# A Fourier mixing layer and a SoLU feed-forward on one Trainium2 core: when the last chunk of a batch pair is transformed, and the order of work in the opening

## Chip, core and metric

One core of a Trainium2 chip runs the whole program. The metric is the device time of one execution in microseconds (us). Engines: TensorE (PE, its weight loads PEld), VectorE (DVE), ScalarE (ACT), GpSimd (POOL) and SyncE (SP), which here only issues DMAs.

## What is computed

```python
X = np.fft.fft(np.fft.fft(x, axis=1), axis=2).real      # x: (8, 3136, 256) float32
h = X.reshape(25088, 256) @ w_in                          # w_in: (256, 1024)
e = np.exp(h - h.max(-1, keepdims=True))
solu = h * e / (e.sum(-1, keepdims=True) + 1e-9)
ln = (solu - mean(solu)) / np.sqrt(var(solu) + 1e-6) * g_ln   # over the 1024 features
out = ln @ w_out                                          # w_out: (1024, 256)
```

The weights arrive as 64-bit floats and are turned into 32-bit floats on the chip.

## The kernel before, in words

**Tiling.** The eight batches go in four pairs (`Pair`, p = 0 to 3, called the first to the fourth). The sequence of 3136 is split as 49 x 64. A pair is loaded in eight chunks (`load`, L117): SyncE brings `xa`, GpSimd's indirect DMA brings `xb`, the rows of the mirrored positions; the last chunk has one more row, `x0`. `add_mirror` (L136) adds the two and `fold` or `fold_part` (L152, L164) adds and subtracts mirrored features into `y`; columns 0 and 128 of `y`, its edges, are copied. `transform1` (L184) does one half of a chunk: four matmul instructions into a PSUM bank (six for the last half, which has `x0` too), a ScalarE copy to `z`, and after a chunk's second half a DMA of `z` to `zd` in DRAM (`keep`). `turn` (L226) reads `zd` back as `g`, five of the 25 values of k1 at a time, in four DMAs.

**Units.** A unit is one k1 of one pair; there are 100 of them, `units[i]`, and the main loops run one step i per unit. `transform2` (L234) makes q of unit i + 2 from g in step i, and `spread` sends one row of it as `r` over SyncE. `up` (L267) multiplies q with Wi (w_in after the feature transform) into two PSUM tiles; `even` (L275) and `join` (L281) on VectorE make h and its extreme, `expo` (ScalarE), `product` (VectorE), `square` (ScalarE) follow. `turn_both` transposes 32 x 32 blocks on VectorE, and `move_blocks` (L396) moves the blocks of two units with 16 DMAs on SyncE in every even step. Five steps later (`lag`) the unit is multiplied with w_out in seven half-size products (`Down`), whose sums GpSimd makes a step ahead (`sums`, L433). `power`, `store` and the loads of later chunks are on GpSimd's queue too; each engine works through its instructions in the order in which they are written.

**Order of the next pair's work.** While a pair's units run, the next pair is loaded and transformed. `SUMS` (L698) holds for each pair the step at which each chunk's mirror begins: f + 2c, with f = 3, 27, 53 for pairs 1, 2, 3. In `ahead` and `ahead_pe` the step a = i - SUMS[p][c] decides: mirror halves at a = 0 and 1, fold halves at 1 and 2, the load of chunk c + 2 at 2, the two halves of `transform1` at 3 and 4. GpSimd's mirrors and sums wait (`behind`) for VectorE's last product, since both read two operands from SBUF. `turn_parts` issues g's first part of pair p in step 25p - 4.

**Opening.** Before unit 0 the first pair goes through without units beside it: the loop at L761 takes the eight chunks, mixed with the conversion of w_in (four pieces: `exponent_in`, `confine`, `narrow_in`) and later w_out (four pieces: `exponent_out`, `confine`, `narrow_out`). `confine` takes three ScalarE instructions (or two of VectorE with `here`). `product_in(h)` (L654) multiplies the feature transform with w_in: h = 0 even half, h = 1 odd half, h = KD the middle column (`w_mid`), and copies the result from PSUM to SBUF by ScalarE. Steps 0 to 4 (`WHOLE`) have a loop of their own (L840), with TensorE transposes in place of block moves.

Of the kernel before, what the change touches and what calls it, by code (L numbers as in the profile page):

```python
# [25 lines left out]
CH = 4  # L26
NC = NH // CH
# [16 lines left out]
def kernel(  # L44
# [19 lines left out]
    nc = tc.nc  # L64
# [3 lines left out]
    KD = D // P  # L68
# [83 lines left out]
    def fold(pr, c):  # L152

        xa, _, x0 = pr.raw.pop(c)
        pr.y[c] = xpool.tile([PR, CH, D], FP32, tag="y", name="y")
        sides = [(pr.y[c], xa)]
        if c == NC - 1:
            pr.y0 = xpool.tile([PR, 1, D], FP32, tag="y0", name="y0", bufs=1)
            sides.append((pr.y0, x0))
        for o, i in sides:  # L160
            fold_features(o, i)
            nc.vector.tensor_copy(out=o[:, :, 0:129:128], in_=i[:, :, 0:129:128])  # L162

    def fold_part(pr, c, part):  # L164

# [447 lines left out]
    class Weights:  # L613
# [40 lines left out]
        def product_in(self, h):  # L654
            ps = ps_h.tile([P, FF], FP32, tag=f"h{h % 2}", name="wps")
            for half in range(2):
                fs = slice(half * HW, (half + 1) * HW)
                for c in range(KD):
                    lhsT = self.m[:, c, :] if h == KD else self.Q[:, c, h * P : (h + 1) * P]
                    nc.tensor.matmul(ps[:, fs], lhsT, self.w_in[c][:, fs], start=(c == 0), stop=(c == KD - 1))  # L660
            nc.scalar.copy(w_mid if h == KD else Wi[:, h, :], ps)

        def place_out(self):
# [31 lines left out]

    SUMS = [None] + [[f + 2 * c for c in range(NC)] for f in (3, 27, 53)]  # L698

    def ahead(pr, i, work, after=None):  # L700

# [12 lines left out]
                          mybir.DependencyInfo(mybir.DependencyClass.Sync, mybir.DependencyReason.DATA),  # L714
                          reason="two operands at a time from SBUF")

    def ahead_pe(pr, i):

        for c in range(NC):
            half = i - SUMS[pr.p][c] - 3  # L720
            if half in (0, 1):
                transform1(pr, c * CH // 2 + half)

# [6 lines left out]
    with tc.manual_schedule():  # L730
        pairs = [Pair(p) for p in range(NP)]
        first, weights = pairs[0], Weights()
# [25 lines left out]
            nc.vector.memset(t, 0.0)  # L758
        weights.exponent_in(0)
        weights.exponent_in(1)  # L760
        for c in range(NC):  # L761

            if c == 0:
                weights.narrow_in(0)
                weights.narrow_in(1)
            elif c < 3:
                weights.narrow_in(c + 1)
            if c < 2:
                weights.exponent_in(c + 2)
            add_mirror(first, c, nc.vector)  # L770
            fold(first, c)
            if c == NC - 1:
                for i in range(3):
                    weights.exponent_out(i)
            if c + 6 < NC:
                load(first, c + 6)
            if c == 3:
                weights.place_out()
                for i in range(2):
                    weights.load_out(i)  # L780
                weights.load_table(0)
                weights.mid()
                weights.scale_out()
            for s in range(CH // 2):
                transform1(first, c * CH // 2 + s)
            if c == 3:
                weights.product_in(0)

        turn(first, 0, nc.sync, 0, 2)
        turn(first, 0, nc.gpsimd, 2, KG)  # L790

        confine(weights.units[0], True)
        for i in range(1, 3):
            confine(weights.units[i])
        weights.product_in(1)
        weights.narrow_out(0)
        weights.exponent_out(3)
        weights.product_in(2)
        for i in range(1, 3):
            weights.narrow_out(i)  # L800

        units = [Unit(p, k1) for p in range(NP) for k1 in range(NK)]
        for t in units[:2]:
            take2(t, transform2(pairs[0], t.k1))
            spread(t)
        confine(weights.units[-1])
        for c in (2, 3, 0, 1, 4, 5, 6, 7):
            keep(first, c, slice(4 * KG, ZR))
        weights.load_table(1)
# [30 lines left out]
        for i in range(whole + 1):  # L840
            cur = units[i]
            prv = units[i - 1] if i else None
            if prv:
                turn_whole(prv)
            for s in cur.signs:
                join(cur, s)
            if prv and i < whole:
                for o, ps in prv.wait:
                    nc.vector.tensor_copy(out=o, in_=ps)
            for s in cur.signs:  # L850
                expo(cur, s)
            if prv and i == whole:
                for o, ps in prv.wait:
                    nc.scalar.copy(o, ps)
            if i == 0:

                weights.narrow_out(3)
            for s in cur.signs:
                product(cur, s)
                if i < whole and s == 0:  # L860
                    square(cur, s)
            if i == 1:
                weights.centre()
                weight_sums()
            if i < whole:

                begin(i + 1)
                if 1 in cur.signs:
                    square(cur, 1)
                stats(cur)  # L870
                power(cur)
            else:
                for s in cur.signs:
                    square(cur, s)
                other_pairs(i, ahead, "mirror", cur)
                turn_both(cur)
                stats(cur)
                power(cur)
            if i == 0:
                turn(first, 1, nc.sync)  # L880
            for work in ("mirror", "fold", "load") if i < whole else ("fold", "load"):
                other_pairs(i, ahead, work)

        def by_seven(i):
# [6 lines left out]
        for i in range(whole + 1, len(units) + lag + 1):  # L891
            cur = units[i] if i < len(units) else None
            prv = units[i - 1] if whole < i - 1 < len(units) else None
            old = units[i - lag] if i < len(units) + lag else None
            seven = by_seven(i - lag)
            kept = units[i - lag - 1] if i >= lag + 1 else None

            if kept:
                store(kept, 0)
            if cur:  # L900
                enter(i)
                even(cur, up(cur, 0))
                cur.odd = up(cur, 1)
                second_transform(i + 2)
            if seven:
                new = Down(old, fresh)
                fresh = False
                new.p1()
                new.seed()
            if i == len(units):  # L910
                for s in prv.signs:
                    square(prv, s)
            if prv:
                stats(prv)
            if seven:
                new.p4()
                new.p5()
                new.keep_p()
            elif old:
                plain = [(s, down(old, s, result(s + 1)[:, 0:D])) for s in old.signs]  # L920
            if cur:
                other_pairs(i, ahead_pe)
            if seven:
                new.p6()
                new.keep_x()
                new.p2()
                new.keep_c()
            elif old:
                for s, ps in plain:
                    scale(old, s, ps)  # L930
            if prv and prv.batch.shared and prv.w:
                prv.batch.mix()
            if cur:
                for s in cur.signs:
                    join(cur, s)
            if seven:
                new.p3()
                new.p7()
                new.finish()
            if cur:  # L940
                other_pairs(i, ahead, "mirror")
            if by_seven(i + 1 - lag):
                sums(units[i + 1 - lag], prv, nc.vector if i > len(units) else nc.gpsimd)
            if i % 2 == 0 and whole < i - 1 < len(units) - 2:
                batches[i // 2 - 1].place()
                move_blocks(batches[i // 2 - 1], slice(0, 2))
            if prv:
                power(prv)
            if kept and 1 in kept.signs:
                store(kept, 1)  # L950
            if cur:
                other_pairs(i, ahead, "fold")
                for s in cur.signs:
                    expo(cur, s)
                for s in cur.signs:
                    product(cur, s)
                if i < len(units) - 1:
                    for s in cur.signs:
                        square(cur, s)
                turn_both(cur)  # L960
                if cur.p == 0 and i in (5, 8, 11):
                    turn(first, (i + 1) // 3)
                for pr in pairs[1:]:
                    turn_parts(pr, i - pr.p * NK)
                other_pairs(i, ahead, "load")
            if i in (len(units), len(units) + 1):
                w = i - len(units)
                if w == 0:
                    batches[-1].place()
                move_blocks(batches[-1], slice(w, w + 1), (nc.sync, nc.gpsimd) if w else (nc.sync,))  # L970
# [82 lines left out]
```

## Time and profile before

| | us |
|---|---|
| median of 3 runs (1149.79 to 1153.33) | 1151.1 |
| profiled execution | 1150.92 |
| its span | 1149.1 |
| TensorE busy | 1098.1 |
| VectorE busy | 993.0 |
| ScalarE, GpSimd busy | 799.3, 799.9 |
| mean granted TensorE clock | 0.994 of full |
| busy TensorE in eleven stretches of 10 us, 0 to 110 | 0.00, 1.96, 5.51, 9.22, 9.43, 9.07, 8.75, 9.61, 8.05, 8.45, 7.05 |

The span runs from the first to the last instruction; the execution's time is 1.8 us longer. In the lines of a timeline the columns are start, length, engine, line of the kernel, operation, output <- input, shape and count; in brackets the idle time of the engine ahead of it and what ended it. In the lines of waits they are engine, tile and line that waited, <- what ended the wait, then total us, count and longest. A queue's own issue of DMAs stands under SPq, or under POOL for GpSimd.

### The profile page before, as it was taken

Reading aid. Unit: us, or ns where it says so; the run is one execution under the profiler, and the core shown is the slowest. Engines: PE = TensorE matmul, PEld = TensorE weight load, DVE = VectorE, ACT = ScalarE, POOL = GpSimd, SP = SyncE. Lnnn points to the kernel's source line nnn. Section 1 sums busy time; section 2 is a strip of 40 time slices with the busy share of each in tenths; the row PEclk is TensorE's granted clock in tenths of the full one; section 3 lists DMA queues with packets and bytes.
Section 4 is the critical chain, followed back from the end, with each engine's and each line's share of the span. In section 5 each row is a group of like instructions: output and inputs, shape, how many; then the busy total and the mean of one; then the engine's idle time right before and its main releaser. Section 6 shows DMA issues by size and latency. Waiting matters only on the chain.

```text
span 1149.1 us, 21936 instructions
## 1 busy us (share of the span) xinstructions
PE 1098.1 (96%) x7026; PEld 877.3 (76%) x7026; DVE 993.0 (86%) x1440; ACT 799.3 (70%) x1945; POOL 799.9 (70%) x698
## 2 busy tenths in 40 slices
PE   2988999999899999999999999999989999999998
PEld 1555787887688778778888787877868778888887
DVE  7889898898789988988888998898878999898983
ACT  4567777777566777777766777777766777777761
POOL 3036788875786888876778788876498576766673
PEclk9999999999999999999999999999999999999999
DMA  9772698776878779966869798876587676865664
GB/s 237 208 193 56 147 193 199 179 150 145 157 162 170 196 171 182 192 152 147 168 142 196 162 193 186 198 178 149 128 149 152 141 158 133 148 142 113 141 138 116
DMA packets 459889, 185.78 MB, mean 162 GB/s; under 512 B 427158, under 2 KB 441758, under 8 KB 459776
## 3 DMA queue, kind: packets, MB, share of 16 engines
q1 hardware_dynamic: 446016, 146.23, 62.1%
q0 software_dynamic: 13760, 38.16, 12.6%
q8 instruction: 57, 0.93, 0.3%
q14 instruction: 56, 0.46, 0.1%
HBM read 44.78 MB, written 38.80 MB: 73 GB/s over the span
## 4 chain that ended last, share of the span: by engine, by line
PE 85%; DMA 5%; DVE 4%; issue 2%; ACT 2%; POOL 1%; SPq 1%; POOLq 0%; DVEq 0%
PE ps_m L446 49%; PE ps_h L272 27%; PE ps_m L216 4%; PE ps_m L244 4%; DMA room<-in_x_dram 2%; DMA g<-zd 1%; DVE h L286 1%; DVE u L301 1%; DMA F<-in_f_tab_dram 1%; ACT h L308 1%; PE wps L660 1%; POOL S L439 0%; DVE ev L278 0%; DVE y L150 0%; DMA zd<-z 0%
## 5 line engine op out<-in xcount | busy, mean ns | idle before, releaser
L272 PE MATMUL ps_h<-Wi,q 128*128 128x512 f32 x800 | 363.3, 596 | 7.7 <-DVE nmax L286 4.5
L439 POOL TENSOR_TENSOR S<-uT 128x512 f32<-128x512 f32 x186 | 240.0, 1290 | 97.4 <-DVE u L301 38.8
L446 PE MATMUL ps_m<-Ws,S 128*128 128x128 f32 x2304 | 297.0, 275 | 0.6 <-POOL xa L142 0.6
L446 PEld LDWEIGHTS ps_m<-Ws,S 128*128 128x128 f32 x2304 | 280.6, 192 | 3.9 <-POOL xa L142 0.7
L308 ACT ACTIVATE h<-u,usum 128x1024 f32<-128x1024 f32 x196 | 225.0, 1149 | 83.6 <-DVE u L301 81.3
L272 PEld LDWEIGHTS ps_h<-Wi,q 128*128 128x128 f32 x800 | 144.7, 191 | 155.4 <-issue 141.5
L301 DVE SCALAR_TENSOR_TENSOR u<-h,u 128x1024 f32<-128x1024 f32 x196 | 239.1, 1256 | 7.2 <-ACT u L294 7.1
L294 ACT ACTIVATE u<-h,nmax 128x1024 f32<-128x1024 f32 x196 | 223.3, 1141 | 8.8 <-DVE nmax L286 5.8
L372 DVE STREAM_TRANSPOSE v<-u 128x2048 f32<-128x2048 f32 x88 | 203.4, 2311 | 3.0
L446 PE MATMUL ps_m<-Wo,uT 128*128 128x128 f32 x1536 | 205.0, 277 | 0.4 <-DMA out_dram<-ot 0.4
L446 PEld LDWEIGHTS ps_m<-Wo,uT 128*128 128x128 f32 x1536 | 188.9, 193 | 1.5 <-issue 1.5
L286 DVE CUSTOM_DVE_ANT_0 h<-ev,ps_h 128x1024 f32<-128x1024 f32 x100 | 122.1, 1221 | 17.3 <-DVE ev L278 8.6
L531 POOL DMA_INDIRECT out_dram<-ot,idx x96 | 109.5, 1141 | 36.5 <-issue 11.3
L286 DVE CUSTOM_DVE_ANT_0 h<-h,ps_h 128x1024 f32<-128x1024 f32 x96 | 117.3, 1221 | 13.8
L278 DVE SCALAR_TENSOR_TENSOR ev<-w_mid,r,ps_h 128x1024 f32<-128x1024 f32 x100 | 124.1, 1241 | 2.9 <-ACT S L589 2.4
L439 POOL TENSOR_TENSOR S<-S,uT 128x512 f32<-128x512 f32 x93 | 120.6, 1297 | 7.3
L439 POOL TENSOR_TENSOR S<-uT,S 128x512 f32<-128x512 f32 x93 | 119.7, 1287 | 7.3
L244 PEld LDWEIGHTS ps_m<-T,g 128*128 128x128 f32 x400 | 60.0, 191 | 60.1 <-issue 55.9
L446 PE MATMUL ps_m<-Ws,uT 128*128 128x128 f32 x768 | 103.6, 279 | 0.0
L446 PE MATMUL ps_m<-Wo,S 128*128 128x128 f32 x768 | 101.5, 275 | 0.8 <-ACT ot L481 0.8
L216 PE MATMUL ps_m<-y,F 98*100 98x258 f32 (+3 forms) x288 | 72.8, 389 | 23.9 <-DVE y L162 23.9
L446 PEld LDWEIGHTS ps_m<-Ws,uT 128*128 128x128 f32 x768 | 95.6, 195 | 0.0
(101 smaller groups left out, 1174.3 us busy)
## 6 DMA issues: line engine op xcount, KB each, us to landing
uT<-v SPq DMA_DIRECT2D x752, 128.0 KB
g<-zd POOLq DMA_DIRECT2D x72, 160.0 KB, 4.6
out_dram<-ot SPq DMA_DIRECT2D x176, 64.0 KB
xa<-in_x_dram SPq DMA_DIRECT2D x28, 392.0 KB
zd<-z SPq DMA_DIRECT2D x24, 400.0 KB
raw_in<-in_moe_w_in_dram SPq DMA_DIRECT2D x4, 512.0 KB
raw_out<-in_moe_w_out_dram SPq DMA_DIRECT2D x2, 1024.0 KB
r<-q SPq DMA_DIRECT2D x100, 0.5 KB
```

Source lines behind the costliest of these rows:

```text
L216: nc.tensor.matmul(o[..., cs], F[:, 2 * t + h, :], i[..., cs], start=first, stop=True, skip_group_check=True)
L244: nc.tensor.matmul(o, g[:, k, h * P : (h + 1) * P], table, start=(h == 0), stop=True, skip_group_check=True)
L272: nc.tensor.matmul(ps[:, fs], t.q[:, c * P : (c + 1) * P], Wi[:, c, fs], start=True, stop=True)
L278: nc.vector.scalar_tensor_tensor(out=t.ev, in0=w_mid, scalar=t.r, in1=ps, op0=ALU.mult, op1=ALU.add)
L286: nc.vector.tensor_tensor_reduce(out=t.h[s], in0=t.h[0] if s else t.ev, in1=t.odd, scale=1.0 if s else -0.5, scalar=3.0e38, op0=ALU.add, o ...
L294: nc.scalar.activation(out=t.u[s], in_=t.h[s], func=ACT.Exp, bias=t.nmax[:, s : s + 1], scale=-1.0, accum_out=t.esum[:, s : s + 1])
L301: t.last = nc.vector.scalar_tensor_tensor(out=t.u[s], in0=t.h[s], scalar=-1.0, in1=t.u[s], op0=ALU.mult, op1=ALU.mult, accum_out=t.usum[:, ...
L308: nc.scalar.activation(out=t.h[s], in_=t.u[s], func=ACT.Square, bias=t.usum[:, s : s + 1], scale=-float(FF), accum_out=t.ssq[:, s : s + 1])
L372: nc.vector.transpose(out=t.batch.v[:, :, t.w], in_=t.both.rearrange("p s (g n) -> p (s g) n", n=32))
L439: i = engine.tensor_tensor(out=S[j], in0=a, in1=b, op=op)
L446: nc.tensor.matmul(o, a[:, c], b[:, c], start=start and c == 0, stop=c == n - 1, skip_group_check=True)
L531: dma = nc.gpsimd.indirect_dma_start(out=out, out_offset=bass.IndirectOffsetOnAxis(ap=idx[:, i : i + 1], axis=0), in_=t.ot[s], in_offset=None)
```

## The change

1. `ahead_pe` takes a flag `late`. For the last chunk the first half is done at a = 3 as before, and the second half in the same step, in a second call placed after the `p2` product and ahead of `mix` and the joins. Other chunks are as before.
2. f of pair 3, the fourth pair, becomes 52.
3. Edge columns of `y` in `fold` are copied by ScalarE, ahead of the feature folds, and no longer by VectorE after them.
4. In the opening's loop the transforms of chunk c - 1 are written after the fold of chunk c; the copy of an input product to SBUF becomes a function of its own (`keep_in`). The even half's product is written in the turn of chunk 4 rather than 3, with `mid` and `scale_out` after it.
5. The middle product precedes the odd one; the odd half's copy to Wi stands between the q copies of units 0 and 1. The first piece of w_out is confined before the third is read.
6. The last piece of w_out is converted with the others, ahead of the first even part, rather than in step 0 between join and product.
7. In step 4 the fold stands ahead of the products rather than after the transposes.

```diff
-    SUMS = [None] + [[f + 2 * c for c in range(NC)] for f in (3, 27, 53)]
+    SUMS = [None] + [[f + 2 * c for c in range(NC)] for f in (3, 27, 52)]
...
-    def ahead_pe(pr, i):
+    def ahead_pe(pr, i, late=False):
         for c in range(NC):
             half = i - SUMS[pr.p][c] - 3
+            if c == NC - 1:
+                half = int(late) if half == 0 else None
+            elif late:
+                half = None
             if half in (0, 1):
                 transform1(pr, c * CH // 2 + half)
...
         for o, i in sides:
+            nc.scalar.copy(o[:, :, 0:129:128], i[:, :, 0:129:128])
             fold_features(o, i)
-            nc.vector.tensor_copy(out=o[:, :, 0:129:128], in_=i[:, :, 0:129:128])
...
             fold(first, c)
-            if c == NC - 1:
-                for i in range(3):
-                    weights.exponent_out(i)
+            if c:
+                first_products(c - 1)
+            if c == 4:
+                weights.keep_in(0, weights.product_in(0))
...
+            if c == 4:
                 weights.mid()
                 weights.scale_out()
-            for s in range(CH // 2):
-                transform1(first, c * CH // 2 + s)
-            if c == 3:
-                weights.product_in(0)
+            if c == NC - 1:
+                for i in range(2):
+                    weights.exponent_out(i)
+                confine(weights.units[0], True)
+                weights.exponent_out(2)
+        first_products(NC - 1)
...
-        confine(weights.units[0], True)
+        middle = weights.product_in(KD)
         for i in range(1, 3):
             confine(weights.units[i])
-        weights.product_in(1)
+        weights.keep_in(KD, middle)
         weights.narrow_out(0)
         weights.exponent_out(3)
-        weights.product_in(2)
-        for i in range(1, 3):
+        confine(weights.units[-1])
+        odd = weights.product_in(1)
+        for i in range(1, 4):
             weights.narrow_out(i)
...
             take2(t, transform2(pairs[0], t.k1))
             spread(t)
-        confine(weights.units[-1])
+            if t is units[0]:
+                weights.keep_in(1, odd)
...
-            if i == 0:
-                weights.narrow_out(3)
+            if i == whole:
+                other_pairs(i, ahead, "fold")
             for s in cur.signs:
                 product(cur, s)
...
-            for work in ("mirror", "fold", "load") if i < whole else ("fold", "load"):
+            for work in ("mirror", "fold", "load") if i < whole else ("load",):
                 other_pairs(i, ahead, work)
...
                 for s, ps in plain:
                     scale(old, s, ps)
+            if cur:
+                other_pairs(i, ahead_pe, True)
             if prv and prv.batch.shared and prv.w:
                 prv.batch.mix()
```

## Prediction

> **What bounds it now.** The busy line comes first, then the waits of TensorE, then the stretches in which it waits.
>
> ```profile
> PE 1098.1 (96%) x7026; PEld 877.3 (76%) x7026; DVE 993.0 (86%) x1440; ACT 799.3 (70%) x1945; POOL 799.9 (70%) x698
> ...
> PE ps_m L216 <- DVE y L162: 23.9, 5, 18.0
> PE ps_m L244 <- DMA g<-zd: 8.9, 2, 4.8
> PE ps_h L272 <- DVE nmax L286: 4.5, 6, 0.9
> PE ps_h L272 <- DVE ev L278: 2.9, 1, 2.9
> ```
>
> TensorE is busy 96% of 1149.1 us and carries 85% of the chain that ended last. A step without a first transform takes it 10.14 us (up at 284.0 to up at 294.1), one with it about 11. So only what makes TensorE wait counts: the opening (until 105 us) and two waits for g. The latter, with all that surrounds the first:
>
> ```profile
> 270.97 13.52 SPq L408 DMA_DIRECT2D uT<-v  x16
> ...
> 288.41 0.47 SPq L224 DMA_DIRECT2D zd<-z  x1
> ...
> 293.05 2.40 POOL L232 DMA_DIRECT2D g<-zd  x4 [10.60 <-DMA zd<-z]
> ...
> 294.11 3.60 PE L272 MATMUL ps_h<-Wi,q 128*128 128x512 f32 x8
> 302.51 0.68 PE L244 MATMUL ps_m<-T,g 128*128 128x128 f32 x4 [4.81 <-DMA g<-zd]
> ...
> 310.91 3.60 PE L272 MATMUL ps_h<-Wi,q 128*128 128x512 f32 x8
> ```
>
> The pair's last zd (step 21) stands on SyncE's queue behind 16 block moves; GpSimd stands 10.6 us in `turn` for it, and TensorE 4.81 us for g. From 294.11 to 310.91 the step takes 16.80 us: 6.66 too many, of which 4.81 are idle and the rest a clock that the records show at 0.77, 0.50 and 0.88 in the three 2 us stretches from 302. The same stands at the start of the fourth pair: 833.74 to 849.80, 16.06 us, 5.92 too many. Between pairs two and three, zd left at 551.18, `turn` at 559.53 did not wait, and TensorE did not either.
>
> **Halves in one step.** For each pair the second half of the last chunk moves a step earlier: six matmul instructions, one z copy (0.59 us) and one 400 KB zd. TensorE's work only changes its step (1.3 us). On ScalarE the copy now stands ahead of mix and expo of step 20: about 1.6 us later for expo, product and the next even part. Even part 21 ended at 279.45 and the join at 282.2, while the next up waits for them at 284.0 and 285.7: 4.5 and 3.5 us of cover. On SyncE zd now waits for that copy (272.8 us) ahead of the 16 moves, which start at 273.4 instead of 271.0; their reader, sums of step 22, starts about 2 us late, and TensorE reads those sums some 11 us later (sums at 265.77, read from 278.19). zd has landed by about 277 (the trace has 3.8 to 4.4 us for these), `turn` is reached near 284, g lands 4.6 to 7.4 us later, by 291.5, and is wanted at 297.6. Both waits go: **-6.66 and -5.92**. Late next is then TensorE itself.
>
> **Fourth pair a step earlier (53 to 52).** All its loads, mirrors, folds and transforms move by one step, an odd number. SyncE's load of the next chunk used to be issued in odd steps, after the moves; now it stands directly behind the 16 moves of an even step. Issue: 2.6 us earlier (674.3 instead of 676.87); mirror: 11 us earlier (672.98 instead of 684.55). By the semaphore events these loads take 7.5 to 9 us. So the mirror, which stood without cover already,
>
> ```profile
> 694.32 2.29 SPq L539 DMA_DIRECT2D out_dram<-ot  x4
> ...
> 697.95 0.34 SPq L125 DMA_DIRECT2D xa<-in_x_dram  x1
> ...
> 706.34 1.27 POOL L142 TENSOR_TENSOR xa<-xa,xb 98x510 f32<-98x510 f32 x1 [1.87 <-DMA xa<-in_x_dram]
> ```
>
> now waits some 6 us for chunks 2 to 7, and 8.6 for chunk 0 (nominal 612.9; its load landed at 621.5). Queued behind it on GpSimd are the four sums (5.1 us), the power and the store. TensorE reads the sums 11 us on, so it is not stopped directly; but the sums then run beside VectorE's fold and products, which also read two operands from SBUF. The nearest row is step 28 of the third pair's loading, where the sums came 4.6 us late:
>
> ```profile
> 362.18 1.45 DVE L149 TENSOR_TENSOR y<-xa 98x254 f32<-98x254 f32 x1
> 363.55 1.25 DVE L150 TENSOR_TENSOR y<-xa 98x254 f32<-98x254 f32 x1
> ...
> 368.98 1.13 PE L446 MATMUL ps_m<-Ws,S 128*128 128x128 f32 x8 [0.58 <-POOL xa L142]
> ```
>
> The two folds took 2.7 us instead of 0.8, and TensorE lost 0.58. Bounds for seven chunks: zero, if the cover holds; and (1.9 for the folds + 2.6 for the products, which took 2.75 and 2.28 at 295 us instead of 2.44 together) x 7 = 32 less VectorE's idle 1.2 us in each of 14 steps = 15. I take the row's 0.58 x 7 = **+4.1**, since it is the same collision in the same place.
>
> The Trainium skill, "SBUF — State Buffer", section "SBUF: two separate sides", speaks against this step: it says that the port pair shared by VectorE and GpSimd is an exclusive lock, held for a whole instruction. By it each of the two folds and two products could lose one whole GpSimd sum of 1.28 us, 5.1 a step, and the estimate would be 36 less 17 = 19 us. The stretched rows agree with the lock; that step's loss on TensorE was smaller.
>
> **Fold of step 4 ahead of its products.** The last wait of the opening:
>
> ```profile
> 98.23 2.31 DVE L372 STREAM_TRANSPOSE v<-u 128x2048 f32<-128x2048 f32 x1
> 100.46 0.60 DVE L149 TENSOR_TENSOR y<-xa 98x254 f32<-98x254 f32 x1
> 100.98 1.72 DVE L150 TENSOR_TENSOR y<-xa 98x254 f32<-98x254 f32 x1
> 102.63 1.23 DVE L174 TENSOR_TENSOR y<-xa,xb 98x2 f32<-98x2 f32 x1
> ...
> 105.11 5.38 PE L272 MATMUL ps_h<-Wi,q 128*128 128x512 f32 x8 [2.95 <-DVE ev L278]
> ```
>
> Even part 5 stands behind a fold of 3.3 us that collides with GpSimd, and TensorE waits for it. Ahead of the products (95.8) the fold finds VectorE idle for 0.45 us; its mirror ends at 95.63, and without collision it takes 0.75, as at 107.74. Products start at 96.45 instead of 95.81, transposes end at 101.1, the even part at 102.35 instead of 105.05. TensorE ends its work at 102.15, so 2.65 of the 2.95 go. The clock, 0.53 and 0.62 from 105 to 109, should then not fall: this step took 13.15, a like one 11.15 and 0.2 for a seed: 1.8 more. **-4.4**; bounds 0 (the mirror comes late) and -4.75.
>
> For the clock the skill ("TensorE: Matmul & The Clock Gate", section "What's actually happening") asks an idle window of about 3.4 us before it falls. The gap here was 2.95 us and it fell; by the page's figure only 2.65 would be won.
>
> **The start.** Nine edge copies leave VectorE. From the last load's wait (36.5 us) four of 0.09 and one of 0.1 are on the path: 0.45. ScalarE takes nine of about 0.2, ahead of z copies of the chunk before; TensorE's transform of chunk 5 starts 0.1 to 0.4 later behind copy of Wi, `mid` and scale, covered by its own waits of 0.19 and 0.39 us at 44.5 and 46.85. The chunk-0 zd goes out at 26.4 at the earliest, and SyncE did not reach it before 28.28. If that cover fails, the 0.45 are lost. The last piece of w_out:
>
> ```profile
> 62.82 0.42 DVE L566 TENSOR_SCALAR S<-raw_out 128x512 int32<-128x512 int32 x1
> ...
> 63.99 1.15 ACT L294 ACTIVATE u<-h,nmax 128x1024 f32<-128x1024 f32 x1 [1.50 <-DVE raw_out L602]
> ...
> 65.47 1.22 DVE L301 SCALAR_TENSOR_TENSOR u<-h,u 128x1024 f32<-128x1024 f32 x1
> ```
>
> Its 2.65 us leave the place before product 0 and fill VectorE's 2.35 us of idle ahead of even part 0: it ends near 59.7, even part 0 started at 60.02. But the exponential did not start at 63.99 because of VectorE: its buffer was free when the zd of z_u landed at 63.9. That zd is issued behind r of unit 1, and its q comes only 0.25 earlier, since ScalarE now copies odd Wi before it. So the product goes from 65.47 to 64.9, not by 2.65: **-0.5** for the whole start, between +0.5 (raw w_out, landed at 47.9, or ScalarE late) and -1. The w_in swap puts 3.4 us of TensorE work after the middle one and changes no sum; w_mid's copy then ends before q 0, which waits for the last confine until 56.75 (57.06 before).
>
> **Sum.** -0.5 - 4.4 - 6.66 - 5.92 + 4.1 = -13.4. The profiled execution took 1150.92 us (span 1149.1), the median 1151.1, so they may be exchanged: **1137.5 us**.
>
> **Rivals.** (a) The fourth pair's late loads cost nothing, TensorE's 11 us hide them: 1133.4. For it: no row shows sums read late without a VectorE collision. (b) They cost 1.5 us a chunk: 10.5, 1144. For it: the mirror waits longer than in the row (6 against 4.6). (c) The opening gives nothing or one g still comes late (SyncE held by zd): 1142 to 1144. (d) Slower: sums and products collide in even and odd steps from 52 to 65, VectorE becomes the bound. Two steps gain 9 and lose 2.4 of cover: 6.6, half of it on TensorE, 3.3 x 7 = 23, 1156.5. It decides from 2.5 us per chunk (17.5 / 7). Against it: a late VectorE lets the load catch up. (e) The change does not do what it says: zd stays behind the moves, about 1150. The program's order of SyncE instructions speaks against it.
>
> **Chances.** Forecast 0.45, (a) 0.25, (b) 0.15, (c) 0.08, (d) 0.05, (e) 0.02. All but (d) and (e) are faster by over 0.3% (3.5 us, about what a measurement can tell from no change). The range runs from (a) less the runs' 1.3 us spread to beyond (b): 1132 to 1147.
>
> **What would show it.** Waits for g gone, both steps near 10.1 us; no wait for even part 5 and its up 3.4 us long; exponential 0 still released by a DMA near 63.7; waits of L142 for xa in even steps 52 to 66, folds above 0.41 us and few TensorE waits there. Wrong if TensorE waits there beyond 10 us in all, or if a g wait stays.

## The result, and the profile after

The changed kernel takes **1155.09 us** (median of 19 runs, 1149.20 to 1161.98) beside 1150.58 us for the kernel before on the same chips: ratio 1.0038, 95% interval 1.0024 to 1.0052. It is slower by 0.4%; the forecast was 1137.5, the range ended at 1147. The profiled execution took 1156.21 us, its span is 1154.3, 5.1 more than before (unrounded).

The busy line of the changed kernel's page, and the longest waits of TensorE:

```profile
PE 1101.5 (95%) x7026; PEld 879.5 (76%) x7026; DVE 1010.4 (88%) x1431; ACT 797.4 (69%) x1954; POOL 799.7 (69%) x698
...
PE ps_m L216 <- ACT y L161: 22.4, 3, 18.6
PE ps_m L216 <- ACT q L250: 7.2, 7, 2.5
PE ps_m L446 <- issue: 5.6, 2, 4.6
PE ps_h L272 <- DVE nmax L286: 4.7, 6, 0.9
```

The waits for g (8.9 us) are gone from the list. Two others have come: a first transform that waits for the copy of q (7.2), and a down product that waits 4.6 at a time. VectorE is busy 17.4 us more with nine instructions less, so its instructions have become longer.

Where the time went is read by marks: the first matmul of `up` of a unit. "54 to 55" below is the time from the mark of unit 54 to that of unit 55.

| us between the marks of units | 0 to 7 | 7 to 25 | 25 to 53 | 53 to 72 | 72 to 99 |
|---|---|---|---|---|---|
| before | 60.22 | 202.79 | 297.23 | 205.33 | 277.29 |
| after | 58.77 | 196.11 | 297.62 | 224.89 | 271.24 |
| difference | -1.45 | -6.68 | +0.39 | **+19.56** | -6.05 |

The span from its start to unit 0, and from unit 99 to its end, differs by -0.06 and -0.60. So one stretch, the loading of the fourth pair, costs more than all the others bring.

The halves did what was forecast. The step in which TensorE used to wait for g, in the timeline of the changed kernel:

```profile
292.60 3.60 PE L272 MATMUL ps_h<-Wi,q 128*128 128x512 f32 x8
296.04 0.61 PE L244 MATMUL ps_m<-T,g 128*128 128x128 f32 x4
...
302.73 3.60 PE L272 MATMUL ps_h<-Wi,q 128*128 128x512 f32 x8
```

The matmuls of `transform2` (L244) follow `up` (L272) with no bracket, so TensorE does not wait for g, and 23 to 24 takes 10.13 us (16.81 before); 73 to 74 takes 10.13 too (16.06). And the costliest step of the fourth pair's loading, again of the changed kernel, the queues and engines in order of time:

```profile
588.67 16.70 SPq L408 DMA_DIRECT2D uT<-v  x16
605.42 1.94 SPq L125 DMA_DIRECT2D xa<-in_x_dram  x2
...
614.84 1.26 POOL L142 TENSOR_TENSOR xa<-xa,xb 98x510 f32<-98x510 f32 x1 [10.48 <-DMA xa<-in_x_dram]
...
616.06 1.26 POOL L439 TENSOR_TENSOR S<-uT 128x512 f32<-128x512 f32 x1
...
617.37 1.16 PE L446 MATMUL ps_m<-Ws,S 128*128 128x128 f32 x8 [1.06 <-POOL S L439]
...
623.00 3.04 DVE L149 TENSOR_TENSOR y<-xa 98x254 f32<-98x254 f32 x1
...
624.48 1.27 POOL L439 TENSOR_TENSOR S<-uT 128x512 f32<-128x512 f32 x1
...
625.96 1.48 DVE L150 TENSOR_TENSOR y<-xa 98x254 f32<-98x254 f32 x1
627.37 1.22 DVE L174 TENSOR_TENSOR y<-xa,xb 98x2 f32<-98x2 f32 x1
...
628.53 2.31 POOL L439 TENSOR_TENSOR S<-uT 128x512 f32<-128x512 f32 x1
...
629.65 2.28 DVE L301 SCALAR_TENSOR_TENSOR u<-h,u 128x1024 f32<-128x1024 f32 x1
...
629.77 1.15 ACT L308 ACTIVATE h<-u,usum 128x1024 f32<-128x1024 f32 x1 [6.23 <-DVE u L301]
...
633.12 0.35 ACT L250 COPY q<-ps_m 128x256 f32<-128x256 f32 x1
633.37 0.27 ACT L472 COPY ps_m<-ps_m 128x128 f32<-128x128 f32 x1
...
633.74 2.04 PE L446 MATMUL ps_m<-Ws,S 128*128 128x128 f32 x8 [4.62 <-issue]
```

Read it from link to link. The pair's first two loads stand behind 16 moves. GpSimd's mirror, nominally at 604.4, stands still for 10.48 us, and its four sums, queued behind, only begin at 616. TensorE waits for them directly, 1.06 and 0.20 us. GpSimd stays behind: its next mirror and sums run from 623.3 to 630.8, beside VectorE's fold and products. The fold's three instructions take 3.04 + 1.48 + 1.22 us instead of 0.41 + 0.42 + 0.16, the second product 2.28 instead of 1.22. ScalarE's squares wait 6.23 us for the products, its copies of q and of the seed stand behind the squares, and the product that needs the seed ("issue" in the bracket: the profile names no releaser) starts as soon as the seed is copied. The clock column of the 2 us windows (window, length, busy, granted clock, DMA share, GB/s), same kernel:

```profile
628.00:630.00 2.00, 1.12 (x11) 1.00 0.74 152
...
632.00:634.00 2.00, 0.26 (x1) 0.50 0.22 68
634.00:636.00 2.00, 2.00 (x10) 0.50 0.03 0
636.00:638.00 2.00, 2.00 (x11) 0.50 0.00 0
```

After the stop TensorE works at half clock: eight matmuls of the same shape take 2.04 us there and 1.16 at 617. 54 to 55 takes 17.07 us, 6.93 too many: 4.62 idle and 2.3 of slow clock. It and two others (57 to 58, 63 to 64) carry 6.93 + 4.12 + 4.40 = 15.45 of the 19.56, of which 4.62 + 2.24 + 2.52 = 9.38 is idle time and most of the rest slow clock. Over the whole stretch TensorE's waits grew from 0.88 us to 12.71.

### The profile page after: what moved, and what is told of

Same layout as the page of the kernel before. It is cut to its first block, busy times and chain, and to the rows that moved or that the text cites. A ratio compares the mean times of both kernels' runs of the same rounds, so it can differ in the third digit from the quotient of the medians.

```text
span 1154.3 us, 21940 instructions
## 1 busy us (share of the span) xinstructions
PE 1101.5 (95%) x7026; PEld 879.5 (76%) x7026; DVE 1010.4 (88%) x1431; ACT 797.4 (69%) x1954; POOL 799.7 (69%) x698
## 4 chain that ended last, share of the span: by engine, by line
PE 76%; DMA 7%; SPq 7%; DVE 4%; issue 3%; ACT 2%; POOL 2%; POOLq 0%; DVEq 0%; ACTq 0%
PE ps_m L446 45%; PE ps_h L272 23%; SPq L408 5%; PE ps_m L216 4%; PE ps_m L244 3%; DMA room<-in_x_dram 2%; DMA out_dram<-ot 1%; DVE u L301 1%; POOL S L439 1%; PE ps_m L514 1%; DMA r<-q 1%; DMA xa<-in_x_dram 1%; DMA F<-in_f_tab_dram 1%; ACT h L308 1%; SPq L224 1%
## 5 line engine op out<-in xcount | busy, mean ns | idle before, releaser
L272 PE MATMUL ps_h<-Wi,q 128*128 128x512 f32 x800 | 361.9, 594 | 6.7 <-DVE nmax L286 4.7
L439 POOL TENSOR_TENSOR S<-uT 128x512 f32<-128x512 f32 x186 | 243.5, 1309 | 107.7 <-DVE u L301 34.2
L272 PEld LDWEIGHTS ps_h<-Wi,q 128*128 128x128 f32 x800 | 144.0, 190 | 153.8 <-issue 139.9
L142 POOL TENSOR_TENSOR xa<-xa,xb 98x510 f32<-98x510 f32 (+1 forms) x48 | 59.5, 1240 | 65.2 <-DVE u L301 27.5
L244 PEld LDWEIGHTS ps_m<-T,g 128*128 128x128 f32 x400 | 60.2, 191 | 49.3 <-issue 46.4
```

The source lines that it names most:

```text
L244: nc.tensor.matmul(o, g[:, k, h * P : (h + 1) * P], table, start=(h == 0), stop=True, skip_group_check=True)
L272: nc.tensor.matmul(ps[:, fs], t.q[:, c * P : (c + 1) * P], Wi[:, c, fs], start=True, stop=True)
L439: i = engine.tensor_tensor(out=S[j], in0=a, in1=b, op=op)
```

## Experiments

The theory (A in the expectations): the fourth pair's loads in even steps are late, so the mirror is late, so the sums meet VectorE, so ScalarE and TensorE are late. Spans of single profiles scatter by some microseconds (unit 0 alone started between 55.84 and 59.83 us), so the stretch from unit 53 to 72 is compared: 205.33 before, 224.89 after. Where no time is given, the run is one profiled execution.

**Back to 53.** The change with one number undone.

```diff
-for f in (3, 27, 52)]
+for f in (3, 27, 53)]
```

> The changed kernel with the fourth pair put back to step 53; halves in one step and the opening stay. Theory A (the loads of the fourth pair, issued in even steps behind 16 block moves, make the mirror late, and the mirror makes GpSimd's sums collide with VectorE): from up of unit 53 to up of unit 71 nothing is lost, the 19.6 us come back, span 1154.3 - 19.6 = 1134.7; the last half is then made in step 70, its zd goes out ahead of that step's moves, so the wait for g at the fourth pair stays away too. Rival B (the loss in those steps belongs to the halves in one step or to the opening's later work, not to the step number): the span stays above 1150. Rival C (step 52 was needed to bring g of the fourth pair in time): 1134.7 + 5.9 = 1140.6.

Measured: span 1136.0, 53 to 72 in 205.33, 72 to 99 in 271.24. Time 1137.44, ratio to before 0.987 (0.9835 to 0.9905). A holds, B and C fall. The lengths of the fold's instructions (minimum/median/maximum in ns, then first and last start) from 585 to 780 us, the changed kernel first, then this one:

```profile
L149 DVE TENSOR_TENSOR y<-xa x13: 411/824/3035, 623.0 to 769.4; 98x254 f32<-98x254 f32 x13
L150 DVE TENSOR_TENSOR y<-xa x13: 410/1478/1493, 626.0 to 769.8; 98x254 f32<-98x254 f32 x13
```

```profile
L149 DVE TENSOR_TENSOR y<-xa x14: 411/414/655, 631.0 to 771.7; 98x254 f32<-98x254 f32 x14
L150 DVE TENSOR_TENSOR y<-xa x14: 411/417/419, 631.4 to 772.0; 98x254 f32<-98x254 f32 x14
```

The median of the fold's second instruction goes from 1.48 us back to 0.42.

**52 alone.** The kernel before with that number only.

> The kernel before with one edit: the fourth pair starts in step 52 instead of 53. Theory A: about +19.6 us between units 53 and 71. The two halves of the last chunk fall in steps 69 and 70, the zd in step 70 goes out ahead of that step's moves, so the wait for g at unit 74 goes (-5.9): span 1149.1 + 19.6 - 5.9 = 1162.8. Rival B (the 19.6 need the other edits as well): 1143 to 1150.

Measured: span 1161.9; 53 to 72 in 225.00, 73 to 74 in 10.13. The cost needs no other edit. And the fourth pair's wait for g goes with either half of the change: in step 70, an even one, zd stands ahead of the moves in any case.

**First loads in step 49.**

```diff
-i == (pr.p - 1) * NK and c < 2 or a == 2 ...
+i == (pr.p - 1) * NK and c < 2 and pr.p < 3 or a == 2 ...
...
+                if i == 2 * NK - 1:
+                    for c in range(2):
+                        load(pairs[3], c)
```

> The changed kernel, but the first two loads of the fourth pair are issued in step 49 (odd, no moves) instead of step 50 (even, behind 16 moves); all later loads stay where the change has them. Theory A: the mirror of step 52 (it waited 10.48 us) no longer waits, and the loss of steps 53 to 56 (1.78 + 6.93 us) goes; the later loads still cost about 10.9: span about 1145.5. Rival D (one late first chunk only starts it, and every later loss follows from it): nearly all 19.6 go, 1135. Rival E (mirrors, folds and sums collide in even steps, however early the load): nothing changes, 1154.

Measured: span 1149.9; 53 to 72 in 217.82, so 12.5 of 19.6 stay. The steps up to the marks of units 54 and 55 are back at 10.13, but those up to 58, 59, 60 and 61 take 12.88, 12.56, 12.28 and 11.62, and that up to 64 takes 17.71. The first chunk's lateness cost what was expected where it stood (8.7); the later chunks then cost 12.5 instead of 10.8 (63 to 64 by 2.3 more, 57 to 58 by 2.2 less): the price of a late load is not a constant per chunk. D and E fall.

**Sums ahead of the mirror** (steps 50 to 74); the loads stay late.

```diff
-            if cur:
+            if cur and cur.p != 2:
                 other_pairs(i, ahead, "mirror")
             if by_seven(i + 1 - lag):
                 sums(...)
+            if cur and cur.p == 2:
+                other_pairs(i, ahead, "mirror")
```

> The changed kernel, but in steps 50 to 74 GpSimd makes the four sums ahead of the mirror instead of behind it; the loads stay late. Theory A (what costs is that the sums are pushed behind a mirror that waits for its load, into VectorE's fold and products): the sums are at their usual place, the loss falls from 19.6 to under 6 us, span 1135 to 1141. Rival E (the late mirror itself is what stretches VectorE, or folds that wait for the mirror): the loss stays above 12 us, span above 1147.

Measured: span 1136.7; 53 to 72 in 207.81, 2.5 of the 19.6 are left. This takes out the middle link alone: it is the order on GpSimd's queue that makes a late load dear. The lengths of the fold's instructions in this kernel, from 585 to 780 us:

```profile
L149 DVE TENSOR_TENSOR y<-xa x15: 411/440/998, 619.7 to 773.8; 98x254 f32<-98x254 f32 x15
L150 DVE TENSOR_TENSOR y<-xa x15: 410/416/1492, 620.5 to 774.1; 98x254 f32<-98x254 f32 x15
```

**xa from GpSimd's queue**, so not behind the moves.

```diff
-nc.sync.dma_start(out=xa, ...
+(nc.gpsimd if pr.p == 3 else nc.sync).dma_start(out=xa, ...
```

> The changed kernel, but GpSimd's queue issues the fourth pair's xa loads, beside its xb loads, instead of SyncE's: they no longer stand behind the 16 moves. Counted from up of unit 53 to up of unit 72 (205.33 us in the kernel before and with the pair at 53, 224.89 in the changed one). Theory A: the loads land earlier, the mirror waits less, and the loss falls from 19.6 to under 8 us; span 1136 to 1143. Rival F (the place on SyncE's queue doesn't matter, the load is late because its buffer comes free late or GpSimd's own issue, 1 us each, takes as much): loss above 14, span above 1148.

Measured: span 1145.5; 53 to 72 in 213.32, 8.0 left. At the edge of A's figure: the place on SyncE's queue is the greater part of it, not all.

**Squares behind the copies.** In steps 53 to 67 `square(prv, s)` is called behind `new.seed()`, and no longer at the end of the step before.

> The changed kernel, but for units 52 to 66 ScalarE makes the squares behind the next step's copies of q and of the seed instead of ahead of them; loads stay late. It tests the last link: late products on VectorE hold ScalarE's squares, these hold the copies of q and seed, and TensorE waits for the copies. If TensorE is stopped by that order of ScalarE's queue alone, the loss from unit 53 to 72 falls from 19.6 to about 3. If VectorE's own lateness is the limit (its even part and join free the banks that up needs), it only falls to some 8 to 14, since VectorE is held 5 us a step in the worst steps whatever ScalarE does. I expect the second: span 1143 to 1149.

Measured: span 1150.8; 53 to 72 in 217.93, 12.6 left, as expected, but for another reason than I gave. In the timeline of this kernel:

```profile
634.62 1.88 PE L446 MATMUL ps_m<-Wo,S 128*128 128x128 f32 x8 [3.36 <-ACT ot L481]
```

q and the seed are now copied in time, and TensorE stops two groups later, for the read of a bank by L481, which still stands behind the squares. So in this step it is ScalarE's queue again and not VectorE's hold on the banks of `up`.

**All loads early**: step 49 for the first two and GpSimd's queue for xa, the two edits above together.

> The changed kernel with the fourth pair still at 52, but none of its loads behind the 16 moves: the first two issued in step 49, and all xa from GpSimd's queue. Each edit alone left 12.5 and 8.0 us of the 19.6 between units 53 and 72. Theory A (only the lateness of the loads costs, the step number itself nothing): at most 2 us are left, 205.3 to 207.3 us between the two units, span 1136 to 1138. Rival E (folds and mirrors in even steps cost something of their own): over 4 us left, 209.5 or more.

Measured: span 1146.1; 53 to 72 in 212.92, 7.6 left. A in its narrow form fails, and the figure lies where rival E put it. In this kernel's timeline:

```profile
613.07 1.28 POOL L439 TENSOR_TENSOR S<-uT 128x512 f32<-128x512 f32 x1 [4.54 <-DMA uT<-v]
```

The mirror no longer waits for its load, but the first sum now waits for the block moves; it does so again at 678.59 (4.55 us) and 769.49 (3.94), each in the step before one that took longer (12.96 and 12.82 us instead of 11.00), while a wait of 2.05 at 744.84 cost nothing. By the semaphore events the moves issued after the marks of units 55, 57, 61 and 63 took 7.3, 9.1, 6.6 and 7.1 us from issue to landing (medians) beside the loads; in the changed kernel it is 5.9, 4.0, 5.2 and 3.5. A load in an even step thus makes the sums late either way, behind the moves through the mirror, beside them through the moves. The first is shown by experiment; the second is read from this trace alone, and nothing was run to part it from E.

**Fold of step 4 alone**, on the kernel before.

> The kernel before with one edit: the fold of step 4 ahead of its products. From up of unit 0 to up of unit 7 the kernel before took 60.21 us, the changed one 58.77. If the late r of unit 2 (1.44 us in step 2) comes from the other edits of the opening, it stays away here: step 5 gives 2.77, step 6 gives nothing (13.2, since TensorE now waits for the join instead of for the even part), 57.45 us from unit 0 to 7, span about 1146.4. If r is late by chance or by this edit: 58.8.

Measured: span 1144.2; 0 to 7 in 57.63; 5 to 6 in 9.69 (12.46 before), 6 to 7 in 13.20, 2 to 3 in 5.88. The fold gives its 2.8 us and no more. (Most of the rest of the span's difference lies in the two waits for g, where 23 to 24 and 73 to 74 took 17.69 and 13.28.)

**Halves and fold on the kernel before**, the start untouched, the pair at 53.

> The kernel before with two edits: halves in one step, and the fold of step 4; pair four at 53, the start as before. Sum by the parts that the traces have shown: -6.67 + 0.4 (third pair) - 5.93 - 2.77 = -15.0: span 1134.1. If the start's other edits (edge columns by ScalarE, last piece of w_out ahead, odd w_in last) do bring something beyond the r that they make late, the kernel with them and step 53 (1136.0) is the faster one.

Measured: time 1136.59, ratio 0.987 (0.984 to 0.9899), as with the start's edits (1137.44, 0.987): no difference to be seen. The profile's span is 1139.9, since unit 0 started at 59.56, 2 to 3 took 7.20 and 29 to 30 took 12.97. So the late r occurs with the start as it was, too.

**Step 53 and the sums ahead of the mirror, and the table behind r.** Two kernels; the second moves `weights.load_table(1)` from ahead of `begin(0)` to behind it.

> The changed kernel with the fourth pair at 53 and the four sums ahead of the mirror in steps 25 to 74. Step 29 to 30 (the third pair's first chunk, whose load is two steps ahead as well) has taken between 10.46 and 14.43 us in ten profiled runs with the same code there. If sums behind a late mirror are what makes it vary, it takes 10.1 to 10.6 here, and the span is that of step 53 less 0 to 1 us in the usual run: 1135 to 1136. Rival: the mirror behind the sums makes the folds late instead, and some step of 27 to 45 or 53 to 69 is longer than 11.1 us.

> As the run before, and SyncE loads the second part of the table T behind r of unit 2 instead of ahead of it. That r landed 6.4 to 7.7 us after its issue and TensorE waited for the even part that needs it. If it was late because it stands behind the table on the queue, units 0 to 5 take about 34.6 us or less instead of 35.9, and the span is 1.2 us shorter than in the run before. If GpSimd's xb load is what holds it, it stays at 35.4 to 35.9.

Measured: the first 1139.69 (ratio 0.9915, 0.9894 to 0.9935), 29 to 30 in 11.89 and 59 to 60 in 11.62; the second 1136.64 (0.9886, 0.9861 to 0.9912), 29 to 30 in 14.64, units 0 to 5 in 34.20 (35.89 in the changed kernel, 35.51 in the first). So with loads that are in time the order of sums and mirror brings nothing, and does not steady 29 to 30; the mirror is not what makes it vary. With the table behind r, units 0 to 5 are as short as expected, in one profile.

**First load of the third pair apart.** Step 53, table behind r, and chunk 0 of the third pair loaded in step 23.

> The changed kernel with the fourth pair at 53, the table behind r of unit 2, and the third pair's first load issued in step 23 instead of beside the second one in step 25. Step 29 to 30 took 10.46 to 14.64 us in thirteen profiled runs; the block moves of step 26 landed 7 to 9 us after their issue in the longest of them, beside those two loads, and 4.6 to 7.5 in a short one. Theory G (two loads at once hold up the block moves that the sums wait for): step 30 takes 11.2 us or less, units 25 to 53 at most 297.4. With units 0 to 5 at 34.6 or less the sum by stretches is 58.0 + 57.1 + 196.1 + 297.0 + 205.3 + 271.2 + 49.3 = 1134.0 for the span. Rival (the moves are late for another reason): step 30 over 12 us.

Measured: **1134.15 us** (1132.57 to 1135.03), ratio 0.9864 (0.9844 to 0.9885), profiled span 1130.8; units 0 to 5 in 34.01, 29 to 30 in 11.15, 25 to 53 in 297.29. It has the lowest ratio of all, though the intervals overlap with that of step 53 alone. One profile with 11.15 doesn't prove theory G: six of the eleven profiles with the old code there had 11.5 or less.

## Why the prediction was wrong, point by point

- **Halves in one step: right.** -6.66 and -5.92 were forecast, -6.68 and -5.93 came (the second comes with step 52 alone, too). "Late next is then TensorE itself" held: the matmuls follow `up` without a wait.
- **Fourth pair a step earlier: this step failed.** "I take the row's 0.58 x 7 = +4.1, since it is the same collision in the same place"; it cost 19.56. The chain up to the late sums was in the text, with the 8.6 us wait of chunk 0 (10.48 measured). Three things were not. First, "TensorE reads the sums 11 us on, so it is not stopped directly" looked at one path from GpSimd to TensorE only; the one that counts goes over VectorE's stretched products to ScalarE's squares, and TensorE waits for what stands behind these: copies of q and seed, and reads of banks. Second, the 11 us were no full cover either: the first late sums stopped TensorE directly for 1.26 us. Third, the three longest stops (4.62, 2.52 and 2.24 us) were each followed by windows at half clock, which the step of the 0.58 row does not contain. The upper bound of 15 counted VectorE alone; the waits grew by 11.8 us, within it, and most of the other 7.7 is slow clock. The prediction's own sign of being wrong, TensorE waits beyond 10 us there, came. Rival (d) with 23 was the nearest, but its even 3.3 us a chunk did not come: three steps carry most of the loss.
- The row itself was a poor price. Its step took 11.10 us, 0.97 more than the 10.13 of a step without a first transform, and not 0.58. And the same step of the third pair took 10.46 to 14.43 us in eleven profiles with the same code there, and over 12.9 in five of them; the one profile at hand happened to be among the short ones.
- **The skill's price.** The measured row comes first: 4.75 us more for a fold, 1.06 for a product, 19.56 for the stretch. The Trainium skill's page "SBUF — State Buffer", section "SBUF: two separate sides", with its exclusive lock between VectorE and GpSimd, had given 19 in the prediction, and I set it aside for the milder row. The lengthened instructions agree with it: 2.63 us more for the first of the fold's three is about two GpSimd instructions of 1.28, and 1.06 more for each of the others is less than one. That the sums agree so well is partly luck, since three steps carry most of the loss and a good part is clock.
- **Fold of step 4: half right.** Of "2.65 of the 2.95", 2.77 came. The 1.8 us for the clock did not: 6 to 7 took 13.15 before and 13.19 after, though the granted clock is now 1.00 throughout. So the prediction's sum without the clock, 2.65, came close for another reason than the one it gave. The opening of the changed kernel:

```profile
79.00 1.98 PE L272 MATMUL ps_h<-Wi,q 128*128 128x512 f32 x4 [1.58 <-DVE ev L278]
...
103.57 1.98 PE L272 MATMUL ps_h<-Wi,q 128*128 128x512 f32 x4 [0.19 <-DVE ev L278]
106.44 1.95 PE L272 MATMUL ps_h<-Wi,q 128*128 128x512 f32 x4 [0.88 <-DVE nmax L286]
```

  The second half of `up` waits for the join, which frees the second bank. Before, the slow first half ended at about 107.8 (half of 5.38 after 105.11), and so did the join: the slow clock lay beside that wait and cost little. I had asked what is late next for the first bank only.
- **The start: the -0.5 can't be read.** Units 0 to 2 gained 0.15 by the earlier product; unit 0 starts where it did, within a scatter of 4 us. The first line above is a loss that I had not seen: r of unit 2 landed 7.7 us after its issue instead of 6.4 and held the even part, 1.29 over units 0 to 5. It can be late with the old start too: the four profiles with that took 34.15, 34.60, 34.74 and 35.90 us from unit 0 to 5, the eight with the new start and the table ahead of r 35.20 to 35.95. So the new start may well delay r. But unit 5 is reached 92.0 to 95.5 us after the span's start with the old start and 92.5 to 94.6 with the new one, which shows neither gain nor loss of the whole. With the table behind r, both profiles have 34.0 to 34.2.
- **Sum.** -1.45 - 6.68 + 0.39 + 19.56 - 6.05 - 0.66 (start and end) = +5.1 for -13.4 forecast; with 4.1 in place of 19.56 it would have been -10.3, inside the range. The missing 3 us lie mainly in the fold's clock and in the start.

## What to carry to other kernels

When a DMA moves to another step, ask what its queue does in that step and what its data shares the engines with, and follow the late result over every engine that meets it, not only to the reader in the program. Price a collision from as many places of the trace as have it: one row is one draw. A wait that goes uncovers the next one on the same operation, so look at each buffer that the operation needs, the second bank too.

## What was not expected of the hardware

- In the fourteen profiles, from 100 us on, nineteen stops of TensorE of 1.93 to 4.86 us came with a granted clock of 0.50, which set in during the stop or within 1.5 us of its end. Three others, of 2.45, 2.91 and 3.01 us, left the clock at 1.00, and no stop under 1.9 us lowered it. So between 1.9 and 3.0 us the length of a stop alone does not decide. The Trainium skill's page "TensorE: Matmul & The Clock Gate", section "What's actually happening", asks for an idle window of about 3.4 us; thirteen of the nineteen were shorter and don't agree.
- The same instructions gave 10.46 to 14.43 us from unit 29 to 30, and in the four kernels with the old start r of unit 2 landed between 5.8 and 7.6 us after its issue: DMA timing differs from run to run by more than some of the effects that were being forecast.
